# First quarter of w_in and w_out converted from float64 during the attention and reloaded as float32 behind the last expert weights

## The chip, the cores and the metric

One core of a Trainium2 chip runs the whole kernel. The metric is the time of one execution in device microseconds (us), the median over several runs.

## What is computed

The reference, cut to what matters:

```python
def _attn_ref(q, k, v):                    # 4 batches, 8 heads, 576 tokens, head dim 64
    q_rot, k_rot = (rotate(q), rotate(k))  # rotary embedding, halves of 32
    scores = scale * np.matmul(q_rot, k_rot.transpose(0, 1, 3, 2))
    scores = scores - np.max(scores, axis=-1, keepdims=True)
    attn = np.exp(scores)
    attn = attn / (np.sum(attn, axis=-1, keepdims=True) + 1e-09)
    return np.matmul(attn, v)

def _moe_ref(x, phi, w1, w2):              # x 2304 x 512, 8 experts of 4 slots, F 1024
    logits = x @ phi
    d = softmax of logits over the tokens;  slot_input = d.T @ x
    for e in range(E):
        h = np.maximum(slot_input[e] @ w1[e], 0.0)
        slot_out[e] = h @ w2[e]
    c = softmax of logits over the slots;   return c @ slot_out

def _moe2_ref(x, w_in, w_out):             # w_in 512 x 2048, w_out 2048 x 512
    r = np.maximum(x @ w_in, 0.0)
    return (r * r) @ w_out
```

All of it is float32, except that w_in and w_out come as float64 (8 MB each); the kernel sees them as pairs of 32-bit words and turns them into float32 itself. w1 and w2 are 16.8 MB each.

## The kernel before, in words

There is no hand-written order. Every step is handed to a planner (`Plan.op`) with the engines that can do it and their costs, a due time, and the keys that it reads and writes. `Plan.emit` simulates the engines and emits, step by step, the one that can start first, with the earlier due time where several can; each engine's order is fixed by that. A transfer's landing is modelled by one shared rate (line 159). Where TensorE (PE) would wait in this model for more than `GAP`, `emit` puts matmuls of the identity into the gap (`fill`, lines 139 to 142 and 1432 to 1435): real instructions, whose results nobody reads. Nearly all transfers are issued by SyncE (SP), whose queue is in order like the others.

**Attention** (16 pairs of heads, ten units of 128 keys by half the queries each). For a pair, q and k are loaded into one of two buffers in the arena (L312), rotated by GpSimd (POOL, L320) and split into a rounded part and its rest. PE forms the scores once for their maxima (L391), which VectorE (DVE) reduces (L398); the row of maxima goes back by a small transfer (L424). It then forms them again at full precision (L443, L447), ScalarE (ACT) takes the exponential (L456), PE multiplies with v (L477). Three pairs of PSUM banks serve as a ring for all of these results. Meanwhile w1 of the first experts is loaded into the ring slots w0 to w9 of SBUF, one slot every 8 units (line 867); w1 of the others and the first w2 go into the attention's own buffers as these come free (A0 to A3, E0, E1, P0 to P2, O0, O1).

**Experts** (two at a time, rounds r = 0 to 3). The first layer (L1089) multiplies the slots with w1; when a w1 tile has been read, `free` (lines 791 to 816) loads the next tile into its slot by the list `LOADS` (lines 678 to 693). The combine weights of the four batches (L889 to L919) are woven in. The second layer (L1150) multiplies with w2, four tiles a round; ACT copies the result (L1165), L1171 sums it, L1186 copies the slots out. The last w2 tiles are those in E0 and E1 (`tEb` and `tEa` in the profile).

**MLP.** The slots are first multiplied with w_in (`w_prime`, L1232 to L1250: PE, ACT, PE, ACT, DVE for each piece of columns); a step of `mlp1` (L1296) then makes 128 features of 768 tokens, ACT and DVE apply Relu and square and split the result (L1307 to L1341), and `mlp2` (L1364) multiplies with w_out. The features are done in four quarters of 12 steps each. Before a quarter, its part of w_in and w_out must be float32: `from_f64` (lines 929 to 983) takes one ACT and four DVE instructions for 1 MB of raw words (L952, L957, L965, L972, L979), and a w_out block is then rounded by ACT (L1266) and its rest taken by DVE (L1271). For the first quarter that is two blocks of w_in (slots A0, A1) and two of w_out (w9, w0), at the end of the experts.

## Time and profile before

| | us |
|---|---|
| median of 3 runs | 623.29 (622.56 to 624.96) |
| the profiled execution | 619.85 |
| its span, first to last instruction | 618.1 |
| PE busy | 584.5 (95%) |
| DVE busy | 385.1 (62%) |
| ACT busy | 279.7 (45%) |
| POOL busy | 215.6 (35%) |

The attention lasts until about 330 us of the span, the two expert layers from 340 to 384, the MLP from there to the end. The busy share of an engine is an average over these stages. A matmul of the program is two records in the trace where its operands are float32 and one where they are rounded (fp32r).

### The profile page before, as it was taken

The page shows a single profiled execution, that of the slowest core. Times are in us where ns is not written, and L with a number is a line of the kernel's source. Part 1 is how long each engine was busy: PE and PEld are TensorE (multiplying, and loading weights), DVE is VectorE, ACT ScalarE, POOL GpSimd, SP SyncE. Part 2 cuts the span into 40 slices and gives each one's busy share as a digit, 9 for nine tenths or more (in the row PEclk, how much of TensorE's full clock was granted, in tenths as well). Part 3 has the DMA queues.
Part 4 walks back from the last instruction along what each step waited for, and adds up shares of the span by engine and source line. Part 5 has one row for each costly group of instructions (what it writes and reads, how often), then busy time and mean ns, then how long its engine had stood idle before and what let it go on. Part 6 is the DMA issues. An engine that isn't in the chain of part 4 may idle for free.

```text
span 618.1 us, 13409 instructions
## 1 busy us (share of the span) xinstructions
PE 584.5 (95%) x5535; PEld 429.8 (70%) x5535; DVE 385.1 (62%) x818; ACT 279.7 (45%) x492; POOL 215.6 (35%) x168
## 2 busy tenths in 40 slices
PE   1899999999999999999997999999999999999997
PEld 1556555565555655555665335899999999999996
DVE  3466666766667666576635526998486569354543
ACT  1234444444344443444441224798584547434340
POOL 2999998538766686671110000000000000000000
PEclk9799999999999999999999999999999999999999
DMA  9536954574366323413438999623220030000222
GB/s 189 135 85 180 225 133 133 151 182 123 108 167 165 80 58 65 99 29 116 174 137 311 335 388 393 254 92 137 69 69 1 1 137 1 1 2 2 103 104 102
DMA packets 36253, 80.90 MB, mean 131 GB/s; under 512 B 7616, under 2 KB 8032, under 8 KB 35168
## 3 DMA queue, kind: packets, MB, share of 16 engines
q1 hardware_dynamic: 34704, 77.98, 41.1%
q10 hardware_dynamic: 1488, 2.06, 1.7%
q8 instruction: 43, 0.70, 0.5%
q14 instruction: 18, 0.15, 0.1%
HBM read 75.24 MB, written 4.72 MB: 129 GB/s over the span
## 4 chain that ended last, share of the span: by engine, by line
PE 55%; POOL 18%; DMA 14%; DVE 5%; issue 3%; SPq 3%; ACT 1%; ACTq 0%; DVEq 0%; POOLq 0%
PE bank L1364 31%; POOL arena L320 12%; DMA arena<-in_qk_dram 11%; PE obank L477 4%; PE bank L443 4%; POOL tLb L320 3%; PE obank L1296 3%; PE bank L1150 2%; SPq L312 2%; PE bank L1089 2%; PE bank L495 2%; POOL tLa L320 2%; DVE mcol L398 1%; DMA arena<-in_rope_dram 1%; POOL pb L464 1%
## 5 line engine op out<-in xcount | busy, mean ns | idle before, releaser
L456 ACT ACTIVATE tO<-bank 128x576 f32<-128x576 f32 (+1 forms) x160 | 99.5, 647 | 157.7 <-PE bank L447 137.6
L398 DVE TENSOR_REDUCE mcol<-bank 128x2 f32<-128x576 f32 x160 | 115.5, 748 | 53.8 <-PE bank L391 53.6
L320 POOL TENSOR_TENSOR arena<-arena 128x576 f32<-128x576 f32 x90 | 125.4, 1414 | 54.2 <-DMA arena<-in_qk_dram 53.9
L477 PE MATMUL obank<-tO,pb 128*64 128x288 f32 x640 | 104.8, 426 | 2.9 <-DVE pb L519 1.6
L1364 PE MATMUL bank<-w,tEb 128*128 128x256 f32 x864 | 106.1, 278 | 1.2 <-ACT w__927 L1380 1.1
L1364 PEld LDWEIGHTS bank<-w,tEb 128*128 128x128 f32 x864 | 103.3, 188 | 3.5 <-issue 1.6
L464 POOL TENSOR_TENSOR pb<-tO 128x576 f32<-128x576 f32 x32 | 45.3, 1418 | 36.8 <-ACT tO L456 36.8
L477 PEld LDWEIGHTS obank<-tO,pb 128*64 128x64 f32 x640 | 34.9, 135 | 31.8 <-issue 17.1
L1364 PE MATMUL bank<-w,tEa 128*128 128x256 f32 x432 | 53.3, 279 | 0.0
L1364 PEld LDWEIGHTS bank<-w,tEa 128*128 128x128 f32 x432 | 51.7, 188 | 1.4 <-issue 1.2
L1364 PE MATMUL bank<-w,tO 128*128 128x256 f32 x432 | 51.3, 276 | 0.0
L1364 PEld LDWEIGHTS bank<-w,tO 128*128 128x128 f32 x432 | 50.9, 188 | 0.0
L501 DVE STREAM_TRANSPOSE bank<-bank 128x288 f32<-128x288 f32 x32 | 15.9, 498 | 44.2 <-PE bank L495 44.2
L1307 ACT ACTIVATE pb<-obank 128x384 f32<-128x384 f32 x47 | 21.7, 493 | 44.8 <-PE obank L1296 44.8
L495 PE MATMUL bank<-tO,ones 128*32 128x288 f32 x384 | 37.5, 410 | 0.0
L443 PE MATMUL bank<-tEb 64*128 64x288 f32 x200 | 35.5, 352 | 0.5 <-ACT tO L456 0.4
L1307 ACT ACTIVATE arena<-obank 128x384 f32<-128x384 f32 x48 | 21.6, 490 | 31.2 <-PE obank L1296 31.2
L443 PEld LDWEIGHTS bank<-tEb 64*128 64x128 f32 x200 | 18.7, 184 | 20.7 <-issue 11.3
L391 PE MATMUL bank<-tEb 64*128 64x288 f32 x200 | 29.6, 334 | 0.7 <-DVE mcol L398 0.5
L443 PE MATMUL bank<-tLb,tEb 64*128 64x288 f32 x200 | 29.5, 292 | 0.0
L443 PE MATMUL bank<-tEb,tLb 64*128 64x288 f32 x200 | 29.5, 291 | 0.0
L320 POOL TENSOR_TENSOR tLb<-arena,tEb 128x576 fp32r<-128x576 f32 x20 | 28.0, 1416 | 0.8 <-ACT tEb L350 0.7
(276 smaller groups left out, 968.9 us busy)
## 6 DMA issues: line engine op xcount, KB each, us to landing
arena<-in_qk_dram SPq DMA_DIRECT2D x15, 576.0 KB
arena<-in_qk_dram SPq DMA_DIRECT2D x14, 512.0 KB
pb<-in_v_dram SPq DMA_DIRECT2D x16, 320.0 KB
arena<-in_w_dram SPq DMA_DIRECT2D x8, 512.0 KB
tLb<-in_w_in_dram SPq DMA_DIRECT2D x3, 1024.0 KB
pb<-in_w_in_dram SPq DMA_DIRECT2D x3, 1024.0 KB
w__415<-in_w_dram SPq DMA_DIRECT2D x4, 512.0 KB
w__591<-in_w_dram SPq DMA_DIRECT2D x4, 512.0 KB
```

The lines of the kernel that those rows point to most:

```text
L320: ENG[e].tensor_tensor(out=o, in0=x, in1=y, op=how)
L391: nc.tensor.matmul(on_ring(tok)[:, j, 0:HQ], lhsT=hi[rows, 1, UNIT[u]], rhs=hi[rows, 0, HALF[h]], start=True, stop=True)
L398: lambda e: nc.vector.tensor_reduce(out=mcol[:, h, :, u], in_=on_ring(tok)[:, :, 0:HQ], op=ALU.max, axis=AX.X),
L443: nc.tensor.matmul(st[:, j, 0:HQ], lhsT=k[x][rows, UNIT[u]], rhs=q[y][rows, HALF[h]], start=(i == 0), stop=False)
L456: lambda e: nc.scalar.activation(out=pr[0:m], in_=on_ring(tok)[0:m, :, 0:HQ], func=AF.Exp, scale=0.125),
L464: lambda e: nc.gpsimd.tensor_tensor(out=acc, in0=one, in1=pr, op=ALU.add),
L477: nc.tensor.matmul(o_t[rows, 0:HQ], lhsT=vr[:, u, j, :], rhs=pr[:, j, :], start=(u == 0), stop=(u == 4))
L495: nc.tensor.matmul(sm[QUAD[2 * j + w], 0:HQ], lhsT=ones[:, 0:32], rhs=xs_[2 * i + w][:, j, :], start=(i == 0), stop=(i == 1))
L501: {"DVE": 0.47}, lambda e: nc.vector.transpose(out=on_ring(tok)[:, 1, 0:HQ], in_=on_ring(tok)[:, 0, 0:HQ]),
L1296: lambda e, i=i, t0=t0: nc.tensor.matmul(BANKS[i][:, 0:384], lhsT=wst_of()[:, 128 * fc : 128 * fc + 128], rhs=cst_of()[:, t0 : t0 + 384], ...
L1307: lambda e, i=i, h=h: nc.scalar.activation(out=rg_of()[:, 0, h], in_=BANKS[i][:, 0:384], func=AF.Relu),
L1364: nc.tensor.matmul(BANKS[c][:, z], lhsT=gt[:, x, 128 * c : 128 * c + 128], rhs=wo[:, fc % 2, y, z], start=(fc % FQ == 0 and i == 0 and z.s ...
```

## The change

`prepare`, called for eight pieces during the attention, loads a piece of 512 KB of raw words into slot w9, converts it with three ACT and two DVE instructions into slot w8, and writes 256 KB of float32 to two tensors in device memory, `wi_single` and `wo_single`. The conversions are `soft`: the planner puts one only where it ends, in its model, before anything more due could start on that engine. The ring slots w0 to w7 are now loaded every 10 units, w8 and w9 after the last piece. Behind the last w2 tiles the two float32 tensors are loaded into A0 and A1 (1 MB each), and `convert_w_in(0, ...)` and the conversion in `convert_w_out(0)` and `(1)` are gone; their rounding stays. The loads of the first quarter's raw words are gone from `LOADS`. Besides, the planner's costs of the experts' matmuls and its rate of transfers are set anew.

```diff
+            if i in self.soft:
+                end = start + self.ops[i][0][e]
+                first = [c for c in cand if c[3] == e and c[2] not in self.soft and self.ops[c[2]][2] < self.ops[i][2] and c[0] < end]
+                if first:
+                    start, _, i, e = min(first, key=lambda c: (self.ops[c[2]][2], c[0], c[2]))
...
-                dma = done = max(end + 1.4, dma) + self.ops[i][4] / 360.0
+                dma = done = max(end + 1.4, dma) + self.ops[i][4] / 385.0
...
-        ("w8", "w2", 6, 1), ("A0", "wi", 0, 0), ("E0", "w2", 7, 0), ("E1", "w2", 7, 1), ("A1", "wi", 0, 1), ("w9", "wo", 0, 0),
-        ("w0", "wo", 1, 0), ("P0", "wi", 1, 0), ("w2", "wo", 2, 0), ("P1", "wi", 1, 1), ("w1", "wo", 3, 0),
+        ("w8", "w2", 6, 1), ("E0", "w2", 7, 0), ("E1", "w2", 7, 1), ("A0", "single", "wi", 0), ("A1", "single", "wo", 0),
+        ("P0", "wi", 1, 0), ("w2", "wo", 2, 0), ("P1", "wi", 1, 1), ("w1", "wo", 3, 0),
...
+    def prepare(i, g):
...
+        dma(
+            lambda: nc.sync.dma_start(out=raw_of().rearrange("p (c f) -> p c f", c=c), in_=src),
+            g, 512, (), [rk], after=pace[g],
+        )
+        u16 = lambda ap, w, k: ap.bitcast(U16).rearrange("p (n w) -> p n w", w=w)[:, :, k]
+        op(
+            {"ACT": 0.66},
+            lambda e: nc.scalar.activation(
+                out=z_of(), in_=raw_of().rearrange("p (n w) -> p n w", w=2)[:, :, 1].bitcast(F32), func=AF.Copy, scale=2.0**-112
+            ),
+            g + 6, [rk], [zk], soft=True,
+        )
+        op(
+            {"ACT": 0.66},
+            lambda e: nc.scalar.activation(out=u16(d_of(), 2, 0), in_=u16(raw_of(), 4, 1), func=AF.Copy, scale=7.49 / 65536),
+            g + 6.1, [rk], [kl], soft=True,
+        )
+        op(
+            {"DVE": 0.4},
+            lambda e: nc.vector.tensor_scalar(
+                out=z_of(), in0=z_of(), scalar1=F64_HUGE, scalar2=-F64_HUGE, op0=ALU.min, op1=ALU.max
+            ),
+            g + 6.1, (), [zk], soft=True,
+        )
+        op(
+            {"ACT": 0.66},
+            lambda e: nc.scalar.activation(out=u16(d_of(), 2, 1).bitcast(F16), in_=z_of(), func=AF.Copy),
+            g + 6.2, [zk], [ks], soft=True,
+        )
+        op(
+            {"DVE": 0.69},
+            lambda e: nc.vector.scalar_tensor_tensor(
+                out=d_of().bitcast(I32), in0=z_of().bitcast(I32), scalar=3, in1=d_of().bitcast(I32),
+                op0=ALU.logical_shift_left, op1=ALU.bitwise_or,
+            ),
+            g + 6.3, [zk, kl, ks], [dk], soft=True,
+        )
+        dma(
+            lambda: nc.sync.dma_start(out=single[kind][:, 512 * j : 512 * j + 512], in_=d_of()),
+            g + 8, 256, [dk, kl, ks], [("hbm", kind, j)], behind=pace[g + 8],
+        )
...
+    PREP = [10 * n + 17 for n in range(8)]
     for n in range(NRING):
-        at(10 + 8 * n, free, f"w{n}", 10 + 8 * n, 2)
+        g = 10 + 10 * n if n < 8 else PREP[-1] + 12 + 8 * (n - 8)
+        at(g, free, f"w{n}", g, 2)
+    at(0.1, stage_bufs)
+    for n, g in enumerate(PREP):
+        at(g + 8.1, prepare, n, g)
...
-                last = op({"PE": 0.95}, m1, g + r + 0.1 * k, [("sit", k // 2)] + here, [("b", bk)])
+                last = op({"PE": 0.52}, m1, g + r + 0.1 * k, [("sit", k // 2)] + here, [("b", bk)])
...
-                op({"PE": 0.95}, m2, g + 10 + r + j / 4, [(ht_k, r)] + wk, [("b", bk)])
+                op({"PE": 0.52}, m2, g + 10 + r + j / 4, [(ht_k, r)] + wk, [("b", bk)])
...
-            op({"PE": 0.75}, ms, g + 10 + r, [hs_k], [("b", 7)], wait=WAIT)
+            op({"PE": 0.55}, ms, g + 10 + r, [hs_k], [("b", 7)], wait=WAIT)
...
-        convert_w_in(0, 0, g - 20)
         convert_w_out(0, g - 10)
-        convert_w_in(0, 1, g - 1)
-        cs[1] = claim("A1", COLS, COLS)
-        (rg1,) = claim("A0", ([128, 2, 2, 384], F32))
+        (rg1,) = claim("w8", ([128, 2, 2, 384], F32))
```

How the orders move, at three places. First PE at the end of the second expert layer (a slot's name is followed by a number; `tEb2` and `tEa2` are the tiles E0 and E1; `ident` rows are fillers; "x4" counts instructions of the program). Before:

```order
L1150 MATMUL bank2_88<-w5__1319,si_66 8x512 x4
L1150 MATMUL bank0_86<-w7__1643,si_66 8x512 x4
L1171 MATMUL obank1_90<-gsum_62,arena_76 128x8 x4
L1150 MATMUL bank0_86<-w8__1804,si_66 8x512 x4
L1435 MATMUL bank1_87<-ident_61 128x128 x4
L1150 MATMUL bank0_86<-tEb2_120,si_66 8x512 x4
L1435 MATMUL bank1_87<-ident_61 128x128 x5
L1150 MATMUL bank0_86<-tEa2_3573,si_66 8x512 x4
L1435 MATMUL bank1_87<-ident_61 128x128 x2
L1171 MATMUL obank1_90<-gsum_62,arena_76 128x8 x4
```

With the change:

```order
L1256 MATMUL obank1_92<-gsum_64,arena_78 128x8 x4
L1235 MATMUL bank0_88<-w7__1983,si_68 8x512 x4
L1525 MATMUL bank1_89<-ident_63 128x128 x4
L1235 MATMUL bank0_88<-w8__691,si_68 8x512 x4
L1525 MATMUL bank1_89<-ident_63 128x128 x11
L1235 MATMUL bank0_88<-tEb2_124,si_68 8x512 x4
L1525 MATMUL bank1_89<-ident_63 128x128
L1235 MATMUL bank0_88<-tEa2_3633,si_68 8x512 x4
L1525 MATMUL bank1_89<-ident_63 128x128 x2
L1256 MATMUL obank1_92<-gsum_64,arena_78 128x8 x4
```

The same four tiles come in the same order; ahead of E1 there are 16 fillers in these rows where there were 9, and five more stand further up (1, 1, 1 and 2, between the products of the third round), where there were none.

Second, ACT at the start of the MLP: L1247 and L1249 (L1334 and L1336 with the change) are the two copies of a w' piece, L1266 (L1357) the rounding of a w_out block. Before:

```order
L1247 ACTIVATE pb_84<-obank1_90 128x128
L1249 ACTIVATE tO1_52_4023<-obank1_90 128x128
L1307 ACTIVATE pb_84<-obank0_89 128x384
L1307 ACTIVATE pb_84<-bank2_88 128x384
L1324 ACTIVATE tEb_49_4039<-pb_84 128x384 x2
L1247 ACTIVATE pb_84<-obank1_90 128x128
L952 ACTIVATE tLa2_119<-w0__415 128x1024
L1249 ACTIVATE tO1_52_4023<-obank1_90 128x128
```

With the change:

```order
L1334 ACTIVATE pb_86<-obank1_92 128x128
L1357 ACTIVATE w9_54_4079<-arena_78 128x2x512
L1336 ACTIVATE tO1_52_4081<-obank1_92 128x128
L1398 ACTIVATE pb_86<-obank0_91 128x384
L1398 ACTIVATE pb_86<-bank2_90 128x384
L1415 ACTIVATE tEb_49_4096<-pb_86 128x384 x2
L1334 ACTIVATE pb_86<-obank1_92 128x128
L1357 ACTIVATE w0_57_4104<-arena_78 128x2x512
L1336 ACTIVATE tO1_52_4081<-obank1_92 128x128
```

The rounding of both w_out blocks now stands between the two copies of a piece; the first of them stood in the second expert layer, and a conversion stood in the second place.

Third, SP's queue during a pair of heads (`mrow` is the row of maxima). Before:

```order
L362 DMA pb_84<-in_v_dram 128x640
L812 DMA w3__927<-in_w1_dram 128x1024 x2
L424 DMA tEb_78<-mrow0_110 1x5x128 x2
L362 DMA pb_84<-in_v_dram 128x640
L312 DMA arena_76<-in_qk_dram 64x2304
```

With the change:

```order
L893 DMA wi_single_93<-w8__691 128x512
L433 DMA tEb_80<-mrow0_114 1x5x128 x2
L856 DMA w9__596<-in_w_in_dram 128x2x512
L823 DMA w3__1081<-in_w1_dram 128x1024 x2
L371 DMA pb_86<-in_v_dram 128x640
L321 DMA arena_78<-in_qk_dram 64x2304
```

The write of a converted piece stands ahead of the row of maxima, the load of the next piece and that of a ring slot behind it, where the ring slot stood ahead.

## Rows read from the trace of the kernel before

**Rows 1.** The page, its first part: busy us, share of the span, instructions.

```profile
PE 584.5 (95%) x5535; PEld 429.8 (70%) x5535; DVE 385.1 (62%) x818; ACT 279.7 (45%) x492; POOL 215.6 (35%) x168
```

**Rows 2.** Busy time by stretch: length, engines (instructions), granted clock, DMA share, GB/s.

```profile
70.00:230.00 160.00, 156.38 (x1678) 93.64 (x1674) 105.72 (x268) 71.37 (x132) 118.94 (x87) 1.00 0.51 131
...
370.00:380.00 10.00, 10.00 (x88) 4.13 (x80) 6.65 (x8) 4.22 (x5) 0.00 (x0) 1.00 1.04 391
380.00:390.00 10.00, 9.33 (x79) 6.72 (x76) 6.94 (x12) 5.13 (x11) 0.00 (x0) 1.00 1.04 399
...
400.00:410.00 10.00, 10.00 (x88) 9.46 (x88) 10.00 (x14) 8.55 (x14) 0.00 (x0) 1.00 0.59 201
```

**Rows 3.** Timeline of PE, expert layers: start us, us, what, [idle before <- releaser].

```profile
340.24 0.62 PE L1089 MATMUL bank<-w__415,sit 128*32 128x512 f32 x2
...
374.20 1.04 PE L1150 MATMUL bank<-w__1319,si 128*8 128x512 f32 x8
375.06 1.04 PE L1150 MATMUL bank<-w__1643,si 128*8 128x512 f32 x8
...
377.99 1.16 PE L1435 MATMUL bank<-ident 128*128 128x128 f32 x8
379.08 1.05 PE L1150 MATMUL bank<-tEb,si 128*8 128x512 f32 x8
380.06 1.38 PE L1435 MATMUL bank<-ident 128*128 128x128 f32 x10
381.37 1.04 PE L1150 MATMUL bank<-tEa,si 128*8 128x512 f32 x8
```

**Rows 4.** Timeline of DVE, the first block of w_out (slot w9).

```profile
375.02 0.77 DVE L957 TENSOR_SCALAR arena<-w__1989 128x1024 uint16<-128x1024 uint16 x1 [0.56 <-DMA w__1989<-in_w_out_dram]
```

**Rows 5.** Timeline of DVE, ACT and PE, from the last slots to the first output matmul.

```profile
379.07 1.06 ACT L1266 ACTIVATE w<-arena 128x1024 fp32r<-128x1024 f32 x1 [2.07 <-issue]
380.16 1.22 DVE L1271 TENSOR_TENSOR w<-arena,w 128x1024 fp32r<-128x1024 f32 x1 [1.17 <-ACT w L1266]
...
384.23 0.29 DVE L1186 COPY sit<-obank 128x128 f32<-128x128 f32 x1 [2.84 <-PE obank L1171]
385.07 0.28 ACT L1247 ACTIVATE pb<-obank 128x128 f32<-128x128 f32 x1 [0.90 <-PE obank L1232]
385.92 0.28 ACT L1249 ACTIVATE tO<-obank 128x128 fp32r<-128x128 f32 x1 [0.58 <-PE obank L1248]
386.73 1.23 DVE L979 SCALAR_TENSOR_TENSOR arena<-tLa,arena 128x1024 int32<-128x1024 int32 x1
389.39 1.62 PE L1364 MATMUL bank<-w,tEb 128*128 128x256 f32 x12
```

**Rows 6.** Timeline of PE, its wait at the first block end.

```profile
411.84 0.39 PE L1364 MATMUL bank<-w,tEb 128*128 128x256 f32 x1 [1.13 <-ACT w__927 L1380]
```

**Rows 7.** Instructions by form, and conversions by line: form xcount, busy us, mean ns.

```profile
L456 ACT ACTIVATE tO<-bank 128x576 f32<-128x576 f32 x128 | 80.9, 650 | 126.4 <-PE bank L447 106.4 <-issue 13.6 <-POOL pb L464 4.2
...
L952 ACT ACTIVATE arena<-tLb x3: 1140/1165/1179, 390.2 to 453.4; 128x1024 f32<-128x1024 f32 x3
L972 DVE TENSOR_SCALAR tLa<-tLa x10: 685/696/708, 372.5 to 515.2; 128x1024 f32<-128x1024 f32 x10
```

**Rows 8.** PE's waits from 50 to 330: us in total, times, longest.

```profile
PE bank L447 <- DMA tEa<-mrow: 2.5, 2, 1.5
PE obank L477 <- DVE pb L519: 1.6, 4, 0.4
PE bank L447 <- DMA tEb<-mrow: 1.6, 2, 0.9
...
PE bank L391 <- DVE r L509: 0.2, 1, 0.2
```

**Rows 9.** POOL's rests by line: ns min/median/max; timeline of DVE there.

```profile
L320 POOL TENSOR_TENSOR tLa<-arena,tEa x12: 1397/1408/1873, 14.5 to 274.5; 128x576 fp32r<-128x576 f32 x12
...
11.58 3.55 DVE L320 TENSOR_TENSOR arena<-arena 128x576 f32<-128x576 f32 x5
```

More of the change, by code (lines that the diff above doesn't have):

```diff
@@ L56, in __init__, with op @@
         self.shared = {}
-    def op(self, engines, fn, due, reads=(), writes=(), kb=None, after=None, spare=None, take=None, give=None, wait=0.0, behind=None, tok=None, mode=None, like=None):
+        self.soft = set()
+    def op(self, engines, fn, due, reads=(), writes=(), kb=None, after=None, spare=None, take=None, give=None, wait=0.0, behind=None, tok=None, mode=None, like=None, soft=False):
         i = len(self.ops)
@@ L81, in op @@
         self.like[i] = like
+        if soft:
+            self.soft.add(i)
         deps.discard(i)
@@ L199 @@
     psum = ctx.enter_context(tc.tile_pool(name="ps", bufs=1, space=PSUM))
+    hbm = ctx.enter_context(tc.tile_pool(name="hbm", bufs=1, space=bass.MemoryType.DRAM))
     SP_ = S + 64
@@ L812, in free @@
                 lambda a=a, z=z: nc.sync.dma_start(out=tile_of()[:, a:z], in_=src[:, a:z]),
-                due + step * i, 1024 / pieces, (), [k], after=pace.get(due, after), behind=behind,
+                due + step * i, 1024 / pieces, [("hbm", key[1], j) for j in range(4)] if key[0] == "single" else (), [k],
+                after=pace.get(due, after), behind=behind,
             )
@@ L816, in free, with stage_bufs @@
         return done
+    single = {kind: hbm.tile([128, WT], F32, name=f"{kind}_single") for kind in ("wi", "wo")}
+    stage = {}
+    def stage_bufs():
+        stage["raw"] = claim("w9", *[([128, 1024], I32)] * 2)
+        bufs = claim("w8", *[([128, 512], F32)] * 4)
+        stage["z"], stage["d"] = bufs[:2], bufs[2:]
+        gen["w8"] = [k for k in gen["w8"]] + [(k, w) for _, k in stage["d"] for w in "ls"]
+        for _, k in stage["d"]:
+            for w in "ls":
+                plan.inherit((k, w), [k])
@@ new lines, in prepare @@
+    def prepare(i, g):
+        kind, j = ("wi", "wo")[i // 4], i % 4
+        (raw_of, rk), (z_of, zk), (d_of, dk) = (stage[x][i % 2] for x in ("raw", "z", "d"))
+        kl, ks = (dk, "l"), (dk, "s")
+        if kind == "wi":
+            r0, c0 = 256 * (j % 2), 512 * (j // 2)
+            src = w_in.bitcast(I32)[r0 : r0 + 256, c0 : c0 + 512].rearrange("(c p) f -> p c f", p=128)
+        else:
+            r0 = 128 * j
+            src = w_out.bitcast(I32)[r0 : r0 + 128, :].rearrange("(c p) f -> p c f", p=128)
+        c = src.shape[1]
+        dma(
[39 more added lines that the diff above has]
+        )
@@ L1097, in experts @@
                 here = [x for i in (k // 2, 2 + k // 2) for x in wk[2 * i + k % 2 : 2 * i + k % 2 + 1]]
-                last = op({"PE": 0.95}, m1, g + r + 0.1 * k, [("sit", k // 2)] + here, [("b", bk)])
+                last = op({"PE": 0.52}, m1, g + r + 0.1 * k, [("sit", k // 2)] + here, [("b", bk)])
                 if k % 2:
                     for sl in wslots[k // 2 :: 2]:
-                        if sl != "A1":
+                        if sl not in ("A0", "A1", "w9"):
                             free(sl, g + r, 2 if where_next(sl) == "w2" else 1, step=0.01)
@@ L1129, in experts @@
             op({"DVE": 0.25}, keep, g + r, [("b", 1 + bk), ht_k], [(ht_k, r)])
-        free("A1", g + 3.5, after=last)
+        for i in range(2):
+            free(f"A{i}", g + 3.5 + 0.1 * i, 2, after=last, step=0.2)
         LATER = (4, 0)
@@ L1156, in m2 @@
                         )
-                op({"PE": 0.95}, m2, g + 10 + r + j / 4, [(ht_k, r)] + wk, [("b", bk)])
-                if wslot[0] != "P":
-                    done = free(wslot, g + 10 + r + j / 4)
+                op({"PE": 0.52}, m2, g + 10 + r + j / 4, [(ht_k, r)] + wk, [("b", bk)])
+                if wslot[0] != "P" and wslot != "w0":
+                    free(wslot, g + 10 + r + j / 4)
                 if wslot in ("w0", "w2"):
-                    free({"w0": "P0", "w2": "P1"}[wslot], g + 10 + r + j / 4, behind=done)
+                    free({"w0": "P0", "w2": "P1"}[wslot], g + 10 + r + j / 4)
             op(
@@ L1201, in mlp @@
         wfs = claim("A3", HALF, HALF)
-        cs[0] = claim("A2", COLS, COLS)
+        of, ks, _ = where["single", "wi", 0]
+        cs[0] = [(lambda k=k: of()[:, 4 * k : 4 * k + 4], ks[k]) for k in range(2)]
+        cs[1] = claim("A2", COLS, COLS)
         gts = claim("tEb", *[([128, 2, 2, 384], F32R)] * 2) + claim("tEa", ([128, 2, 2, 384], F32R))
@@ L1255, in convert_w_out @@
         def convert_w_out(n, due):
-            raw_of, rk, rslot = where[("wo", n, 0)]
-            wf_of, wf_k = wfs[n % 2]
-            f64(wfs[n % 2], raw_of, due, rk, None)
+            if n < 2:
+                of, ks, _ = where["single", "wo", 0]
+                wf_of, wf_k, rslot = lambda: of()[:, 2 * n : 2 * n + 2], ks[n], ("w9", "w0")[n]
+            else:
+                raw_of, rk, rslot = where[("wo", n, 0)]
+                wf_of, wf_k = wfs[n % 2]
+                f64(wfs[n % 2], raw_of, due, rk, None)
             ((wo_of, wo_k),) = claim(rslot, ([128, 2, 2, DM], F32R))
@@ L1416, in mlp @@
             if 0 < i < NQ:
+                if i == 2 and at_ == 0:
+                    cs[0] = claim("A0", COLS, COLS)
                 if at_ in (0, 2):
```

2 lines of the change are left out of this document (added).

## The prediction

> **What bounds the kernel now.** I began with the page's busy times: TensorE is busy for 95% of the span, far above any other engine [rows 1]. So I asked in which stage TensorE does work that is not needed, and in which it waits. The table of stretches [rows 2] says: in the attention (70 to 230) TensorE is at 98%, VectorE at 66%, ScalarE at 45%, GpSimd at 74% and DMA at half. From 370 to 390 DMA is saturated at 391 and 399 GB/s, and TensorE is nearly full as well (10.00 and 9.33 of 10). The reader is to see that both look like the bound there, and only the order of instructions tells which one is.
>
> The timeline of TensorE at the end of the second expert layer settles it [rows 3]. A product with half an expert's w2 takes 0.86 us (374.20 to 375.06). Between the last three stand filler matmuls of the identity (L1435): eight records at 377.99, ten at 380.06. The product with E0 begins at 379.08 and that with E1 at 381.37, each right where the filler ends. Landings I take from VectorE, which waited until 375.02 for the first block of w_out [rows 4]; E0 and E1 are the next 2.1 MB of the queue, at 391 GB/s 5.4 us, so E1 lands near 380.4 (an estimate from these rows). TensorE came to it 1 us later, so the weights no longer decided. From E1 the chain is: copy on ScalarE, L1171, the copy of the slots at 384.23, then the start of the MLP, whose first output matmul comes at 389.39 [rows 5]. From there to the end TensorE waits little: the one wait of the MLP is 1.13 us at 411.84 [rows 6].
>
> **The change, part by part.** *DMA.* 2.1 MB of float64 no longer stand ahead of E0 and E1, so E1 lands near 375.0 instead of 380.4. Singles of 2.1 MB follow and land near 380.4. By itself this is worth nothing: TensorE is then not there yet. What hides it is TensorE's own work of two layers; if that were shorter, rival A would come.
>
> *Fillers, +3.2 us.* The planner's new figures (0.52 us where the row shows 0.86; 385 GB/s) make it believe that TensorE waits longer, and it fills those waits in its model with real instructions. In the second layer ahead of the E1 product 9 fillers stood; now 21 do (1, 1, 1, 2, then 4, 11 and 1). One program filler is two records: 1.09 us for four (377.99 to 379.08) and 1.31 for five (380.06 to 381.37), so 0.27 each [rows 3]. Twelve more are 3.2 us, on TensorE, in order, whatever the weights do. The other matmuls of the two layers are the same in number, only the combine transposes move. Bounds: 0, if each fell into a wait, and 3.2; I take 3.2, since E1 is there 9 us early (375.0 against 381.4 + 3.2).
>
> *Start of the MLP, +0.9 us.* On ScalarE the rounding of the first w_out block (1.05 us, as L1266 [rows 5]) now stands between the two copies of the first w' piece. Before, the second (L1249) began 0.57 us after the end of the first (385.35 to 385.92). Now it cannot begin before 1.05 us are over: +0.5. The difference of that block (1.22 us on VectorE, L1271) then lies ahead of the first square, and fits into the wait for its Relu, within 0.1 us. The second block's rounding does the same to the second piece: +0.4. What goes in exchange is the conversion of the second half of w_in's first quarter (on VectorE until 387.96, in gaps of this chain [rows 5]) and that of the second w_out block. It saves VectorE 3.5 us of the stretch to 410, where it was full [rows 2]; but ScalarE, which held the block end at 411.84 [rows 6], keeps its work: one conversion of 1.17 us goes and one rounding of 1.05 us comes. So I take nothing back there; the bounds are -1.1 (that wait gone) and +1. The conversions of 371 to 379 ran beside the second layer: zero.
>
> *Attention, +1.5 us.* Eight pieces bring 24 ScalarE and 16 VectorE instructions. A piece is half the size of the rows of before: ScalarE 24 x 1.16/2 = 13.9 us, VectorE 8 x (0.69 + 1.23)/2 = 7.7 us [rows 5, 7], 21.6 us in all, put where the planner sees a gap. Cover: ScalarE waited 106.4 us for TensorE before its exps alone [rows 7]. On the path: TensorE's waits for VectorE and ScalarE between 50 and 330 are four rows, from 1.6 down to 0.2 us, 2.9 us together; 2.5 + 1.6 = 4.1 us go to the row of maxima behind other transfers [rows 8]. Bounds: -4.1 (those gone, since the ring weights now go out behind the row and not ahead of it) and +21.6 (nothing covered). I take a value near the lower end, 0.2 us per piece, as the gaps are many; but each piece goes to and fro (ScalarE, VectorE, ScalarE, VectorE), and a late step holds an in-order queue with exps and maxima behind it. The 4 MB read and 2 MB written there are hidden: DMA is half idle. On SP's queue the write of a piece stands ahead of a row of maxima, but its last VectorE instruction comes well before that row's: zero. The conversion's buffers are the ring slots w8 and w9, filled later; they are first needed in expert 4: zero.
>
> *Sum.* 3.2 + 0.9 + 1.5 = +5.6 us on the profiled execution of 619.85 us, so 625.4. That execution is 3.4 us below the median of the runs, 623.29; to the median the same sum gives **628.9 us**.
>
> **Rivals.** *A, faster: the weights set the end.* If in truth the products waited for their weights and the fillers lay in that wait, the E1 product would follow the landing: 375.0 instead of 381.4, so -6.4 + 0.9 + 1.5 = -4.0, 619.3 us. It decides if the E1 product starts less than 41.1 us after the first product of the layers (340.24 to 381.37). For it speaks the saturated DMA; against it that a product takes 0.86 us with tiles loaded long before, too, and that fillers are unconditional. Chance 0.12.
>
> *B, much slower: VectorE and GpSimd hold each other up.* GpSimd's first instruction of the program began at 14.5, while a two-input VectorE instruction in SBUF ran (until 15.13), and took 1.873 us against a median of 1.408 [rows 9]: it was stretched by 0.47 us, about as long as the other still ran. If the pair excludes each other, each of the 16 new VectorE instructions, all SBUF to SBUF, finds GpSimd busy in 74% of cases and waits half of 1.41 us, 8.3 us in all, and holds GpSimd for its own 7.7 us; half of the 16 us reaching TensorE, through late maxima and through the q and k loads that GpSimd releases, makes +8 in place of +1.5: 623.3 + 12.1 = 635.4 us. For it is that one row; against it only that VectorE itself is a third idle. Chance 0.17. The Trainium skill has it as a rule (SBUF — State Buffer, "SBUF: two separate sides"): the two engines share a port pair as an exclusive lock, which a VectorE instruction in a two-port mode or with two SBUF inputs takes for its whole length. By that rule the trace agrees in its one case, 1.873 us; the sum would be B's.
>
> *C, no change: the attention gives back what the fillers take.* The row waits go (-4.1), the wait at 411.84 too (-1.1), conversions cost 1.0: 3.2 + 0.9 - 4.1 - 1.1 + 1.0 = -0.1, 623.2 us. For it: SP's new order; against it that all row waits but the later pairs' must come from the ring loads. Chance 0.21.
>
> **Numbers.** My forecast has 0.50, its own range 626 to 633 (attention from -1 to +5). The range of all reaches from 620.5, past C, to 635; left out are A (0.12) and the upper half of B (0.08). A measurement of this kernel can tell about 0.5% from no change, 620.2 to 626.4 us. Faster: A, 0.12. Same: C and 0.03 of the forecast's low edge, 0.24. Slower: the rest and B, 0.64.
>
> **What would show it.** From the first product of the first layer to the copy of the slots: 44.0 us before (340.24 to 384.23), 47.2 after by the fillers; under 42 is A. From that copy to the first output matmul: 5.2 before, about 5.8 after. Ahead of the E1 product 42 filler records stand where there were 18. The first product comes 1.5 us later than 340.24 by my term for the attention, 8 by B (with GpSimd instructions above 1.5 us in 60 to 230), earlier by C. The E1 tile would be waited for by nobody. If the layers take 47 us but the whole is no slower, my attention or MLP term is wrong; if they take 44 or less, the fillers are.

## The result and the profile after

The changed kernel takes 630.72 us (628.09 to 631.73) where the kernel before takes 623.29: the ratio is 1.0105, interval 1.0076 to 1.0135. It is slower, by 7.4 us; the forecast was 628.9 with its own range 626 to 633. The time came out inside the range. Of the three terms of the sum two were 1 us or more too small (fillers, attention) and one 0.8 us too large (start of the MLP), so their errors cancelled in part. The profiled execution took 631.73 us, 11.9 more than that of the kernel before (619.85). Its time is divided here at four instructions: the first product of the expert layers (L1173), the product with E1 (L1235), the copy of the slots (L1271) and the first output matmul (L1455). All times are in us, from one profiled execution each; the later columns are experiments told below:

| | before | the change | again (e5) | e1 | e9 | e12 |
|---|---|---|---|---|---|---|
| start to first product | 340.24 | 347.84 | 342.62 | 343.10 | 340.11 | 337.85 |
| first product to product with E1 | 41.13 | 45.21 | 46.79 | 39.09 | 39.28 | 47.22 |
| first product to copy of the slots | 43.99 | 48.20 | 49.78 | 42.08 | 43.46 | 50.21 |
| copy to first output matmul | 5.16 | 5.25 | 5.25 | 5.24 | 5.17 | 5.25 |
| from there to the end | 228.71 | 228.61 | 228.65 | 228.58 | 228.66 | 229.29 |

So +7.6 us came before the layers, +4.2 in them and nothing after them. The second execution of the same kernel (e5) has only +2.4 before the layers, and e1, which has the same instructions up to there, +2.9. The first execution had two stretches of lower granted clock there (next rows), but e1 had two as well (0.75 from 65 to 70, 0.78 from 335 to 340), so they don't explain the other 5 us; what does stays open. The page's first part of the change, to be held against [rows 1]:

```profile
PE 595.3 (95%) x5561; PEld 435.8 (69%) x5561; DVE 390.8 (62%) x817; ACT 290.8 (46%) x513; POOL 219.3 (35%) x168
```

The stretches of the change (columns as in [rows 2]):

```profile
65.00:70.00 5.00, 3.48 (x28) 2.08 (x26) 4.15 (x12) 1.70 (x3) 3.71 (x4) 0.93 1.08 273
70.00:75.00 5.00, 5.00 (x46) 3.20 (x46) 1.42 (x2) 3.31 (x6) 5.00 (x4) 0.73 0.95 298
...
70.00:230.00 160.00, 154.18 (x1620) 91.29 (x1622) 120.57 (x274) 84.51 (x151) 118.83 (x84) 0.99 0.61 165
...
335.00:340.00 5.00, 2.31 (x29) 1.89 (x24) 3.38 (x12) 0.43 (x1) 0.00 (x0) 0.90 0.65 245
340.00:345.00 5.00, 4.62 (x36) 3.10 (x36) 1.44 (x5) 1.91 (x9) 0.00 (x0) 0.76 1.05 389
```

Between 70 and 230 VectorE has 14.9 us more work than in [rows 2] (120.57 against 105.72), ScalarE 13.1 more and TensorE 2.2 less. TensorE stood still for 1.5 us from 65 to 70, and then the granted clock fell: it is 0.73 on average from 70 to 75, that is, in part of this stretch TensorE ran at the lower of its two levels, 1.2 instead of 2.4 GHz. The same came again at 335 to 345 (0.90, 0.76), where TensorE stood still for 2.7 us first. In e5 TensorE stood still for 1.0 us from 65 to 70 and for 2.7 from 330 to 335, and the granted clock stayed at 1.00 in both places.

TensorE's timeline of the change in the layers, which answers to [rows 3]:

```profile
347.84 0.62 PE L1173 MATMUL bank<-w__427,sit 128*32 128x512 f32 x2
...
389.00 2.72 PE L1525 MATMUL bank<-ident 128*128 128x128 f32 x22
391.66 1.04 PE L1235 MATMUL bank<-tEb,si 128*8 128x512 f32 x8
392.63 0.49 PE L1525 MATMUL bank<-ident 128*128 128x128 f32 x2
393.05 1.05 PE L1235 MATMUL bank<-tEa,si 128*8 128x512 f32 x8
```

The 42 filler records stand where they were forecast, in seven places; the last two places are the rows L1525. From the first filler of a place to the next product they take 6.3 us in all (2.66 of them from 389.00 to 391.66). No product waits for E0 or E1.

TensorE's waits of the change from 50 to 340, which answer to [rows 8]:

```profile
PE obank L486 <- DVE pb L528: 2.7, 7, 0.4
PE bank L547 <- DVE pb L528: 2.7, 1, 2.7
PE bank L400 <- DVE mcol L407: 2.2, 4, 0.7
PE bank L452 <- DVE mcol L407: 1.7, 5, 0.6
PE bank L504 <- ACT tO L465: 1.7, 2, 0.9
PE bank L456 <- DMA tEb<-mrow: 0.4, 1, 0.4
PE bank L456 <- DMA tEa<-mrow: 0.3, 1, 0.3
```

The 4.1 us for the row of maxima shrank to 0.7, as rival C had it. In their place stand 3.9 us for VectorE's maxima (mcol, L407) and 1.7 for an exp, which before were 0.7 and 0.4. One wait was turned into others. (e5, the same code, has 2.2 for maxima and 2.2 for an exp there.)

What VectorE's new instructions met is seen in three places of the timelines of VectorE and GpSimd of the change:

```profile
96.81 0.68 DVE L886 SCALAR_TENSOR_TENSOR w__691<-w__691 128x512 int32<-128x512 int32 x1
...
167.82 1.41 POOL L329 TENSOR_TENSOR arena<-arena 128x576 f32<-128x576 f32 x1
168.18 1.34 DVE L874 TENSOR_SCALAR w__691<-w__691 128x512 f32<-128x512 f32 x1
...
210.16 1.95 POOL L329 TENSOR_TENSOR tLb<-arena,tEb 128x576 fp32r<-128x576 f32 x1
210.17 0.68 DVE L886 SCALAR_TENSOR_TENSOR w__691<-w__691 128x512 int32<-128x512 int32 x1
```

GpSimd's instruction ends at 169.23 and the clamp (L874) at 169.52, 0.29 later, though it had begun 1.05 before that end. All eight clamps end 0.28 or 0.29 us after a GpSimd instruction ends. The merge (L886) takes 0.68 us where GpSimd is idle (96.81). At 210.17 the merge was not held, and GpSimd's instruction beside it took 1.95 us instead of 1.41, 0.54 more. The eight of each line by min, median and max (ns):

```profile
L874 DVE TENSOR_SCALAR w__691<-w__691 x8: 549/1098/1499, 73.3 to 207.4; 128x512 f32<-128x512 f32 x8
L886 DVE SCALAR_TENSOR_TENSOR w__691<-w__691 x8: 675/1702/1950, 77.2 to 210.2; 128x512 int32<-128x512 int32 x8
```

They are 8.6 and 11.1 us in all. If 0.28 and 0.68 us are their undisturbed lengths, they would be 8 x 0.28 + 8 x 0.68 = 7.7 (an estimate: no clamp ran without GpSimd beside it). By it twelve us of VectorE are waiting.

The start of the MLP, ScalarE of the change, answering to [rows 5]:

```profile
396.87 0.28 ACT L1334 ACTIVATE pb<-obank 128x128 f32<-128x128 f32 x1 [2.05 <-PE obank L1319]
397.05 1.05 ACT L1357 ACTIVATE w<-arena 128x1024 fp32r<-128x1024 f32 x1
397.99 0.27 ACT L1336 ACTIVATE tO<-obank 128x128 fp32r<-128x128 f32 x1
```

From copy to copy it is 1.12 us where it was 0.85 (385.07 to 385.92): +0.27, not +0.5.

### The profile page after: what moved, and what is told of

Read it like the earlier page. It is cut to its first block, busy times and chain, and to the rows that moved or that the text cites. A ratio compares the mean times of both kernels' runs of the same rounds, so it can differ in the third digit from the quotient of the medians.

```text
span 629.9 us, 13502 instructions
## 1 busy us (share of the span) xinstructions
PE 595.3 (95%) x5561; PEld 435.8 (69%) x5561; DVE 390.8 (62%) x817; ACT 290.8 (46%) x513; POOL 219.3 (35%) x168
## 4 chain that ended last, share of the span: by engine, by line
PE 60%; POOL 13%; DMA 13%; DVE 5%; ACT 3%; issue 3%; SPq 2%; ACTq 0%; DVEq 0%; POOLq 0%
PE bank L1455 29%; DMA arena<-in_qk_dram 10%; POOL arena L329 8%; PE obank L486 6%; PE bank L452 5%; PE bank L504 3%; PE bank L1235 2%; POOL tLb L329 2%; PE bank L1173 2%; PE obank L1387 2%; DVE mcol L407 2%; SPq L321 2%; PE bank L400 2%; PE bank L456 1%; POOL tLa L329 1%
## 5 line engine op out<-in xcount | busy, mean ns | idle before, releaser
L407 DVE TENSOR_REDUCE mcol<-bank 128x2 f32<-128x576 f32 x160 | 115.3, 748 | 38.4 <-PE bank L400 37.2
L1455 PE MATMUL bank<-w,tEb 128*128 128x256 f32 x864 | 106.1, 278 | 0.6 <-ACT w__1081 L1471 0.6
L1455 PEld LDWEIGHTS bank<-w,tEb 128*128 128x128 f32 x864 | 103.3, 188 | 2.9 <-issue 1.6
L1455 PE MATMUL bank<-w,tEa 128*128 128x256 f32 x432 | 53.5, 279 | 0.0
L1455 PEld LDWEIGHTS bank<-w,tEa 128*128 128x128 f32 x432 | 51.9, 188 | 1.4 <-issue 1.2
L1455 PE MATMUL bank<-w,tO 128*128 128x256 f32 x432 | 51.3, 276 | 0.0
L1455 PEld LDWEIGHTS bank<-w,tO 128*128 128x128 f32 x432 | 50.9, 188 | 0.0
L452 PE MATMUL bank<-tEb 64*128 64x288 f32 x200 | 36.1, 356 | 1.8 <-DVE mcol L407 1.4
L1398 ACT ACTIVATE w__691<-obank 128x384 f32<-128x384 f32 x48 | 21.6, 488 | 34.6 <-PE obank L1387 34.4
L504 PE MATMUL bank<-tO,ones 128*32 128x288 f32 x384 | 37.5, 410 | 0.0
L452 PEld LDWEIGHTS bank<-tEb 64*128 64x128 f32 x200 | 19.1, 186 | 21.5 <-issue 8.9
L400 PE MATMUL bank<-tEb 64*128 64x288 f32 x200 | 30.8, 340 | 1.8 <-DVE mcol L407 1.7
L400 PEld LDWEIGHTS bank<-tEb 64*128 64x128 f32 x200 | 17.6, 184 | 17.4 <-issue 6.2
```

Source lines behind the costliest of these rows:

```text
L400: nc.tensor.matmul(on_ring(tok)[:, j, 0:HQ], lhsT=hi[rows, 1, UNIT[u]], rhs=hi[rows, 0, HALF[h]], start=True, stop=True)
L407: lambda e: nc.vector.tensor_reduce(out=mcol[:, h, :, u], in_=on_ring(tok)[:, :, 0:HQ], op=ALU.max, axis=AX.X),
L452: nc.tensor.matmul(st[:, j, 0:HQ], lhsT=k[x][rows, UNIT[u]], rhs=q[y][rows, HALF[h]], start=(i == 0), stop=False)
L504: nc.tensor.matmul(sm[QUAD[2 * j + w], 0:HQ], lhsT=ones[:, 0:32], rhs=xs_[2 * i + w][:, j, :], start=(i == 0), stop=(i == 1))
L1398: lambda e, i=i, h=h: nc.scalar.activation(out=rg_of()[:, 0, h], in_=BANKS[i][:, 0:384], func=AF.Relu),
L1455: nc.tensor.matmul(BANKS[c][:, z], lhsT=gt[:, x, 128 * c : 128 * c + 128], rhs=wo[:, fc % 2, y, z], start=(fc % FQ == 0 and i == 0 and z.s ...
```

## The experiments

Ratios are to the kernel before, run on the same chip each time (its medians there were 620.6 to 621.8 us); 0.001 is 0.62 us.

**e1: the change without its fillers ahead of E1.**

```diff
-                    if r == 2:
+                    if r == 3 and j == 3:
                         spare_bank[:] = [BANKS[2][:, 0:128]]
```

> The change, with the 21 fillers (42 records) ahead of the product with E1 left out; every other instruction keeps its place. In the profile of the change these fillers take 6.3 us of TensorE between the products (the product with E1 starts 45.2 us after the first product of the layers). If they are plain TensorE work (my theory), the product with E1 comes 6.3 us earlier, 38.9 us after the first product, and the time is 630.7 - 6.3 = 624.4 us, give or take 1. If they only fill waits for weights that land late (rival A), the start stays at 45.2 us and the time at 630.7. If TensorE's granted clock falls without them, something between, with a clock under 1.00 in the rows of 370 to 400.

1.0016 (0.9998 to 1.0033), 621.66 us. This is 624.3 us on the scale of the first measurement, where 624.4 was expected. The copy of the slots comes 42.08 us after the first product, 6.1 earlier, with the last products back to back and the granted clock at 1.00 throughout the layers:

```profile
378.62 1.06 PE L1256 MATMUL obank<-gsum,arena 128*128 128x8 f32 x8 [0.78 <-ACT arena L1250]
...
380.48 1.04 PE L1235 MATMUL bank<-w__691,si 128*8 128x512 f32 x8
381.33 1.04 PE L1235 MATMUL bank<-tEb,si 128*8 128x512 f32 x8
382.19 1.04 PE L1235 MATMUL bank<-tEa,si 128*8 128x512 f32 x8
```

No product waits for E0 or E1 here either. The fillers of the change are plain work, but for the two ahead of L1256: without them TensorE waits 0.78 us there for ScalarE. Rival A falls for the changed kernel.

**e9: the kernel before without its nine.** The same edit in the kernel before.

> The kernel before, with only its 9 fillers (18 records, 2.4 us) ahead of the product with E1 left out; nothing else moves. By the prediction E1 landed 1 us before TensorE came to it, so the product would start 40.1 us after the first product instead of 41.1, and the kernel gains 1.0 us (0.9984 of before). If the fillers lay in a wait for weights almost wholly (40.66 in the kernel before with the planner's 385 GB/s, which has none either), it gains 0.2 to 0.5 us (0.9992 or more). If they were plain work, 2.4 us (0.9961).

0.9986 (0.9970 to 1.0003): by the time no difference from 1 can be told, and only the last of the three expectations is excluded. In the profile 2.4 us of fillers gone brought the copy of the slots only 0.5 us forward (43.99 to 43.46), and the reason is seen in TensorE's timeline:

```profile
377.74 1.33 PE L1150 MATMUL bank<-tEb,si 128*8 128x512 f32 x8
379.39 1.03 PE L1150 MATMUL bank<-tEa,si 128*8 128x512 f32 x4 [0.32 <-DMA tEa<-in_w_dram]
380.75 1.03 PE L1150 MATMUL bank<-tEa,si 128*8 128x512 f32 x4 [0.33 <-DMA tEa<-in_w_dram]
```

E1's second half is waited for until 380.75. In the kernel before the fillers lay in the wait for the weights, but for 0.5 us.

**e2: the change without VectorE's 16 instructions; e3: without ScalarE's 24 as well.** In e2 the two operations on VectorE issue nothing, and in e3 none of the five does (two short memsets on VectorE stand in their place); every other instruction keeps its place.

```diff
-            lambda e: nc.vector.tensor_scalar(
-                out=z_of(), in0=z_of(), scalar1=F64_HUGE, scalar2=-F64_HUGE, op0=ALU.min, op1=ALU.max
-            ),
+            lambda e: None,
```

> The change, without the 16 VectorE instructions of the conversion during the attention (the clamp and the merge of the eight pieces are left out, so the singles hold other values); the planner still reckons with them, so all other instructions stand in the same order on every engine. In the profile of the change they take 19.7 us of VectorE where they would take some 10 undisturbed (8 x (0.55 + 0.68)). If their length beside GpSimd is what makes maxima late (rival B of the prediction), the first product of the layers comes 4 to 6 us earlier than 347.8 and the time is 625 to 627 us. If the attention lost its time to another order of TensorE's instructions (the planner's new figures), the first product stays within 1.5 us of 347.8 and the time is 629.5 to 631.

> The change, with all 40 ScalarE and VectorE instructions of the conversion during the attention left out (two short memsets in their place, the stored values are zeros); the loads and stores of the eight pieces stay, and so does the order of everything else. If ScalarE's 24 instructions cost as much as VectorE's 16, 2 us or more less than without VectorE's alone; if they lie in gaps (they follow exps that TensorE waits for in few places), within 1 us of it. What is left of the attention's loss against the kernel before (first product at 340.2) is then the order and the DMAs: by the theory of the order 4 us or more, by the theory of the conversions under 1.5.

e2: 1.0069 (1.0048 to 1.0091), 625.59 us. e3: 1.0079 (1.0055 to 1.0104), 626.01 us. Against the change (e5, next) VectorE's instructions cost 0.0040, 2.5 us, give or take 2, between the two expectations; ScalarE's cost nothing that can be measured. The first product of e2 comes at 340.03: 7.8 us before that of the first execution, more than either expectation said, but 2.6 before e5's. That of e3 comes at 342.52, with two stretches of lower clock ahead of it, and decides nothing. The layers of e2 take 48.19 us, as in the change.

**e5: the change again.**

> The changed kernel itself, on the same chip as the three that follow and the kernel before, so that their differences need no second chip. With the ratio measured first (1.0105) it stands 6.5 us above the kernel before. On the account so far (layers +4.2, VectorE's conversion about +2, order and DMAs about +1) it is +6 to +7.5 us; if VectorE's part were nothing, +5.

1.0109 (1.0084 to 1.0134), 627.96 us, 6.7 above the kernel before on this chip, as expected. In the profiled execution the granted clock is 1.00 from 60 to 75, but 0.83 from 370 to 380, in the layers, although TensorE was busy throughout from 370 to 375: the lower level comes at another place. At the first filler the layers are 0.7 us behind those of the first execution, at the second place of fillers 1.6 us: that is why they took 49.78 us here.

**e4: the kernel before with the planner's 385 GB/s alone.**

```diff
-                dma = done = max(end + 1.4, dma) + self.ops[i][4] / 360.0
+                dma = done = max(end + 1.4, dma) + self.ops[i][4] / 385.0
```

> The kernel before with a single figure changed: the planner's DMA rate, 360 to 385 GB/s. This alone moves instructions of TensorE in the attention from the fourth pair on (as the change does, whose order differs from before's at the same place first), and it also takes away the 9 fillers (18 records, 2.4 us) ahead of the product with E1. If the order is what cost the attention its time, the first product comes 3 to 5 us later than 340.2, with a stretch of lower granted clock near 70 us as in the profile of the change; if not, within 1 us of 340.2. In the layers: if the weights land at 380.4 as I estimated, the product with E1 starts 40.2 us after the first product, and not 41.1 - 2.4 = 38.7. Time by order: 623.3 + 4 - 1 = 626; without: 622.3.

1.0001 (0.9981 to 1.0020): no difference, and the first product at 339.30, no later than before. Both numbers that were expected with the order as the cause failed. By itself the figure's order costs nothing that can be told. On the weights this run says nothing, against its expectation: the product with E1 starts 40.66 us after the first, but TensorE waited for ScalarE before it, and two of the nine fillers were still ahead of it (e9's expectation, that there were none, is wrong too):

```profile
376.50 1.06 PE L1171 MATMUL obank<-gsum,arena 128*128 128x8 f32 x8 [1.34 <-ACT arena L1165]
...
379.32 0.71 PE L1435 MATMUL bank<-ident 128*128 128x128 f32 x4
```

**e12 and e7: the planner's figure back at 360 in the change, with fillers and without.** The diff of e4 turned round; e7 has that of e1 too.

> The change with the planner's DMA rate alone back at 360 GB/s. It brings 30 fillers ahead of E1's product in place of 21 (60 records in 7 gaps; at the 6.3 us that 42 took in 7 gaps, some 8.5 us: +2.2). If the order of the attention that 385 GB/s makes costs 4 to 5 us by itself, as the pair without fillers says (1.0016 and 0.9943, on two chips): 1.0109 - 0.0073 + 0.0035 = 1.007. If that difference was the chip's, or holds only without fillers: 1.014. The first product comes before 341 by the former.

> The change without the fillers ahead of the product with E1 and with the planner's DMA rate back at 360 GB/s, so that the attention's order is nearer to that of the kernel before. If the figure's order costs about 1 us of the attention, this is 1 us faster than the change without fillers (1.0016 of before): 0.998 to 1.001 of before; if the order costs nothing, 1.0015 again, give or take 0.002. The copy of the slots is 42 us after the first product of the layers either way.

e12: 1.0052 (1.0032 to 1.0072), somewhat less than its first expectation (1.007), though the planner put in 30 fillers for 21 and the copy of the slots came 2.0 us later (50.21). e7: 0.9943 (0.9914 to 0.9973), 616.82 us, faster than both kernels and than either of its expectations. With the pieces in the attention, the figure costs 0.0057 and those 2.0 us, 5.5 us, in the first pair (the change and e12), and 4.5 us in the second (e1 and e7). Among the waits of e12 from 50 to 340 there is none for a row of maxima, and late maxima cost only 0.7 us:

```profile
PE obank L486 <- DVE pb L528: 3.2, 8, 0.4
PE bank L547 <- DVE pb L528: 2.7, 1, 2.7
PE bank L504 <- DVE mcol L407: 0.7, 1, 0.7
```

(e7, the same code in the attention, has one more wait for maxima, of 1.5 us. Behind the layers e12 and e7 take 0.6 us longer than the change: 229.29 and 229.31.) One thing that differs is in the timeline of TensorE at 67 us. First the change, where a score matmul waits for a maximum there and the row sums (L504) come at 73.41:

```profile
67.29 0.40 PE L452 MATMUL bank<-tEb 64*128 64x288 f32 x2 [0.64 <-DVE mcol L407]
...
73.41 0.43 PE L504 MATMUL bank<-pb,ones 128*32 128x288 f32 x1
```

Then e12, with the row sums at 67.06, as in the kernel before (L495 there, at 66.83):

```profile
67.06 0.40 PE L504 MATMUL bank<-pb,ones 128*32 128x288 f32 x1 [0.74 <-DVE mcol L407]
```

By itself this is not what costs the time: e4, which is no slower than the kernel before, has its row sums late too, behind the same wait for a maximum (0.64 at 66.17):

```profile
71.01 0.43 PE L495 MATMUL bank<-pb,ones 128*32 128x288 f32 x1
```

**e10: e7 without VectorE's 16.** The edit of e2 in e7.

> The change without the fillers ahead of E1's product and with the planner's 360 GB/s (0.9943 of before), now also without the 16 VectorE instructions of the conversion in the attention (the clamp and the merge are left out); the order of all else stays. If VectorE held up by GpSimd costs 2.4 us whatever the order (625.6 against 628.0 with the planner's 385): 0.990 to 0.991. If the order at 360 leaves room for it: 0.993 to 0.995.

0.9902 (0.9882 to 0.9923), as expected by the first of the two accounts: against e7 VectorE's instructions cost 0.0041, 2.5 us, give or take 2, here too. The start of the last row of maxima tells how far the attention is, free of what comes behind it. It follows from the timelines of VectorE, in the order: before, e4, e2, e5, e12, e7, e10.

```profile
306.36 0.28 DVE L419 TENSOR_SCALAR mrow<-bank 10x128 fp32r<-10x128 f32 x1 [0.68 <-PE bank L414]
```

```profile
305.42 0.28 DVE L419 TENSOR_SCALAR mrow<-bank 10x128 fp32r<-10x128 f32 x1 [0.68 <-PE bank L414]
```

```profile
306.17 0.28 DVE L428 TENSOR_SCALAR mrow<-bank 10x128 fp32r<-10x128 f32 x1 [0.69 <-PE bank L423]
```

```profile
308.74 0.28 DVE L428 TENSOR_SCALAR mrow<-bank 10x128 fp32r<-10x128 f32 x1 [0.68 <-PE bank L423]
```

```profile
303.99 0.28 DVE L428 TENSOR_SCALAR mrow<-bank 10x128 fp32r<-10x128 f32 x1 [0.69 <-PE bank L423]
```

```profile
305.13 0.28 DVE L428 TENSOR_SCALAR mrow<-bank 10x128 fp32r<-10x128 f32 x1 [0.69 <-PE bank L423]
```

```profile
302.45 0.28 DVE L428 TENSOR_SCALAR mrow<-bank 10x128 fp32r<-10x128 f32 x1 [0.68 <-PE bank L423]
```

In these seven no stretch of lower clock lies between 30 us and this row. e12 and e7 have the same instructions up to it and differ by 1.1 us, so a difference of two such times is good to about 1 us. Read in pairs: VectorE's conversions cost 2.6 us at 385 (306.17 to 308.74) and 1.5 or 2.7 at 360 (302.45 to 303.99 or 305.13). Without them, e10 is 3.9 us ahead of the kernel before (306.36 to 302.45), and its list of waits has none for a row of maxima, where rival C had 4.1 to gain. The figure 385 takes 3.7 of it back where the pieces stand in the plan (302.45 to 306.17), and takes nothing where they don't (305.42).

Most of these 3.7 us lie in one place. From the row of maxima at 228 us to the next e2 takes 21.1 us (228.00 to 249.06) and e10 18.2 (227.90 to 246.14). TensorE of e2 waits there for a row and for an exp:

```profile
235.64 0.59 PE L456 MATMUL bank<-tEa,pick 64*128 64x288 f32 x2 [1.56 <-DMA tEa<-mrow]
...
242.20 0.43 PE L504 MATMUL bank<-pb,ones 128*32 128x288 f32 x1 [1.20 <-ACT tO L465]
```

e10, e12, e7 and e11, all at 360, have neither of these two waits there; every run at 385 has both (e4: 0.37 and 1.06).

**e8: the planner told the true lengths, without fillers.**

```diff
-            {"DVE": 0.4},
+            {"DVE": 1.08},
...
-            {"DVE": 0.69},
+            {"DVE": 1.39},
```

> The change without the fillers ahead of the product with E1, and with the planner's costs for the clamp and the merge set to the means that the profile of the change shows (1.08 and 1.39 us in place of 0.40 and 0.69). If VectorE's held-up conversions cost time because the planner puts them into gaps that are too short, they now find longer ones: maxima are waited for less (2.2 + 1.7 us in the profile of the change) and the time is 0.997 to 1.000 of before. If gaps of that length don't exist, 1.0015, give or take 0.002.

1.0041 (1.0025 to 1.0057): the first expectation is excluded, and the second (1.0015, give or take 0.002) only just met. Telling the planner the true lengths gained nothing; against e1 this order of the same pieces is 1.6 us slower, give or take 1.5.

**e6: the clamp at every second value (first the even ones, then the odd).**

```diff
-                out=z_of(), in0=z_of(), scalar1=F64_HUGE, scalar2=-F64_HUGE, op0=ALU.min, op1=ALU.max
+                out=z_of().rearrange("p (n w) -> p w n", w=2), in0=z_of().rearrange("p (n w) -> p w n", w=2), scalar1=F64_HUGE, scalar2=-F64_HUGE, op0=ALU.min, op1=ALU.max
```

> The change, with the eight clamps reading and writing every second value in turn (the same values, another order); all instructions keep their places. In the profile of the change every clamp ends 0.28 us after a GpSimd instruction ends, whenever it began: 0.55 to 1.50 us long. If it is held because it runs at two values a cycle (0.28 us for 512 values), at one value a cycle it is not held: about 0.6 us each, wherever GpSimd stands, and the kernel is 0.5 to 1.5 us faster than the change. If every VectorE instruction that reads and writes SBUF alone is held, the clamps are 0.8 to 1.8 us long and the time is the same or 0.5 us longer. The merges, with two inputs in SBUF, stay as they were under both.

1.0114 (1.0084 to 1.0144), the same. The clamps are held as before:

```profile
L874 DVE TENSOR_SCALAR w__691<-w__691 x8: 506/1260/1586, 71.1 to 203.5; 128x512 f32<-128x512 f32 x8
```

This is inconclusive: the shortest began at 71.10 and ended 0.3 us after the GpSimd instruction that had begun at 69.89 (1.42 long), as all eight did, so the stride did not slow the clamp to the 0.6 us that were expected of it, and whether its speed is what has it held stays open.

**e11: e7 with the clamps on GpSimd.**

```diff
-            {"DVE": 0.4},
-            lambda e: nc.vector.tensor_scalar(
+            {"POOL": 0.9},
+            lambda e: nc.gpsimd.tensor_scalar(
```

> The change without the fillers ahead of E1's product, with the planner's 360 GB/s, and with the eight clamps on GpSimd itself, where nothing can hold them up. In the profile of the change they took 8.6 us of VectorE, 6.4 of these held. If VectorE's hold-up is what costs: 0.991 to 0.993 of before. If GpSimd's own queue, which feeds q and k to TensorE, is the tighter one, the 8 x 1 us there make row maxima and scores later: 0.995 or more.

0.9926 (0.9901 to 0.9950), also faster than both kernels. It lies where the first expectation put it, but can't be told apart from e7 (0.9943), and the planner's order is no longer e7's: whether VectorE's waiting or just its new work costs the 2.5 us is not shown. A clamp takes 0.61 us on GpSimd, every time:

```profile
L874 POOL TENSOR_SCALAR w__705<-w__705 x8: 606/613/632, 73.3 to 199.5; 128x512 f32<-128x512 f32 x8
```

## Why the prediction was right, and where it was not

**DMA, worth nothing by itself: wrong by some 1.4 us.** The landing of E1, estimated at 380.4, was 380.75 at most (e9). But from this it was read that TensorE came 1 us after the weights, so that they no longer decided. The nine fillers were the cover of a wait: without them TensorE waits for E1. Without fillers on either side the change is 1.4 us quicker through the layers (43.46 to 42.08). Rival A had the right mechanism for the kernel before, and the wrong end, since the change brought new fillers.

**Fillers, +3.2: right in kind, +4.2 in size.** The number (42 records) and their being unconditional are shown by e1. The term was mis-sized. The price of 0.27 each came from places of four and five; the 21 cost 6.1 us, 0.29 each, since four of the seven places hold a single program filler, which takes 0.41 to 0.42 us to the next product, while the two ahead of L1256 cost nothing (e1). And the nine were taken at their 2.4 us, of which only 0.5 were on the path. So 6.1 - 0.5 is 5.6 where 3.2 was forecast; less the 1.4 us of the DMA term it is +4.2, as measured. The two errors partly cancel.

**Start of the MLP, +0.9: wrong, 0.1.** The rounding does stand between the copies of the first piece, but costs 0.27 us there, since it begins 0.10 us before the first copy's recorded end and the second copy 0.11 before its own. VectorE then gives 0.2 of it back: its step behind the second copy (L1244, L1331 with the change) begins 0.31 us after that copy began where it was 0.49, since in the kernel before VectorE was still in a conversion. First the kernel before, then the change:

```profile
385.69 0.69 DVE L972 TENSOR_SCALAR tLa<-tLa 128x1024 f32<-128x1024 f32 x1
386.41 0.29 DVE L1244 TENSOR_TENSOR tO<-obank,tO 64x128 fp32r<-64x128 f32 x1
```

```profile
398.30 0.29 DVE L1331 TENSOR_TENSOR tO<-obank,tO 64x128 fp32r<-64x128 f32 x1 [1.97 <-ACT tO L1336]
```

The +0.4 for the second piece was no addition: a conversion of 1.17 us had stood where the rounding of 1.07 now stands, and with the change the first output matmul (401.29) doesn't wait for that copy (401.82). The wait at 411.84 [rows 6] went from 1.13 to 0.55 us, and no time came of it. Copy to end is 233.87 before and 233.86 after.

**Attention, +1.5: +2.5 to +3.2 by the medians, from parts of other sizes.** This is 6.7 us (e5) or 7.4 (the first measurement) less 4.2. The 0.2 us a piece is what e10 and e12 give (1.5 us over eight); e10 and e7, and the change's own order, give 0.3. The reason given, ScalarE and VectorE to and fro, is not borne out: ScalarE's 24 cost nothing that can be measured (e3), and VectorE's are held by GpSimd. What the step left out is the planner's new DMA figure, which it used for the fillers alone. That figure orders the attention as well, and there, together with the pieces, it costs 3.7 to 5.5 us, about what the rows of maxima had given (3.9). That the sum came out near the measured time is in part luck: a gain and a cost of about 4 us, neither of them in it, cancelled.

**Rival B: mechanism right, price wrong.** The signs named for it are there: GpSimd's instructions above 1.5 us, such as the twelve of this row of the change from 60 to 235, 1.52 in the mean where it was 1.42 before:

```profile
L329 POOL TENSOR_TENSOR tLb<-arena,tEb 128x576 fp32r<-128x576 f32 x12 | 18.1, 1520 | 0.2 <-ACT tEb L359 0.2
```

VectorE waited 12 us, not 8.3. But of this and the 7.7 us of work only 2.5 reached TensorE, not 8. That the rest lay in VectorE's own idle time is argued, not shown. The first product 7.6 us late would have been taken for B; e5, with 2.4 at the same code, and e1, with 2.9, show that some 5 us of it belonged to that one execution. The rule that was cited from the Trainium skill (SBUF — State Buffer, "SBUF: two separate sides"), that whichever starts first keeps the port pair for its whole instruction and the other fully blocks, agrees with these runs both ways: the clamp at 168.18 waits for GpSimd, and GpSimd loses 0.54 us to the merge of 0.68 us at 210.17. Its condition, a two-port mode or two inputs in SBUF, no run here tells apart.

**Rival C: its gain exists** (e10 is 3.9 us ahead, with no wait for a row left of the 4.1 us), and the order took it back. Which part of the change took the rows' waits away was not varied by itself.

What stays open is why the order made with 385 GB/s hurts only with the pieces in it. The late row sums are not the reason by themselves (e4), nor are the nine waits for maxima of the first execution: e2, without VectorE's pieces, has one of them left (0.6 us) and is still 3.7 us behind e10. The waits of e2 at 235.64 and 242.20 show where 2.8 of the 3.7 us go, but no run took these two away by themselves.

## What to carry to other kernels

Work that a planner puts into gaps of its model (filler matmuls here) is real work as soon as the model's gap isn't there: when transfers come earlier, look first at what fills the wait for them. One constant of a scheduler can reach every stage; change its figures one at a time and split the time at instructions that all versions have. The version to keep (e7) has the quarter converted in the attention, no fillers ahead of E1 and the planner's old DMA figure: 0.9943 of the kernel before.

## What the runs showed of the hardware

VectorE's SBUF-to-SBUF clamp of 128x512 float32 never ended before a GpSimd instruction that was running when it began had ended: each of the eight took 0.55 to 1.50 us and ended 0.28 or 0.29 us after GpSimd's did, and at stride 2 they ended 0.28 to 0.29 us after it as well (0.51 to 1.59 us). On GpSimd the same clamp takes 0.61 us. The granted clock fell to 0.73 in a stretch of five microseconds behind 1.5 us in which TensorE stood still (65 to 70), in one execution of a kernel and not in another (e5, 1.0 us), where it fell in the layers instead, with TensorE busy. In e4 TensorE stood still for 1.5 us from 65 to 70, too, and the granted clock stayed at 1.00.
